# Top-k attention and a squared-ReLU feed-forward: ScalarE makes the masks, and the last batch runs by row groups

## The chip, the cores and the metric

The kernel runs on one core of a Trainium2 chip. The metric is the device time of one execution in microseconds (us). A core has five engines that each work through their own instruction list in order: TensorE (PE, matrix products), VectorE (DVE), ScalarE (ACT), GpSimd (POOL) and SyncE (SP, which here issues every DMA). They wait for each other by semaphores, so a waiting instruction holds up all that stands behind it on its engine.

## What is computed

Attention over 8 batches of 8 heads with 576 tokens of width 64, in which each query keeps only its 32 largest scores, followed by a feed-forward over the 4608 tokens of width 512:

```
scores = scale * np.matmul(q, k.transpose(0, 1, 3, 2))
kth    = np.partition(scores, -32, axis=-1)[..., -32:-31]
scores = np.where(scores >= kth, scores, -1e9)
attn   = exp(scores - max) / sum(exp(scores - max))
x      = (attn @ v), heads side by side     # [4608, 512]
r      = np.maximum(x @ w_in, 0.0)          # w_in  [512, 2048]
out    = (r * r) @ w_out                    # w_out [2048, 512]
```

## The kernel before

Heads are taken in pairs, so there are 8 batches of 4 pairs. The 576 query rows of a pair make 9 blocks of 128 rows (4 per head, and one block with the last 64 rows of both heads): 288 blocks in all. Blocks are worked in groups of 2, 2, 2 and 3, so a pair has 4 groups and the program 128.

**Search.** TensorE makes a block's scores in f32 (64x288 products), ScalarE copies them to SBUF as tile `s` (L482). The 32nd largest of 576 is found in two halves: `m` is the maximum of the two halves (VectorE, L510), `lo` the minimum, made on GpSimd from integer sums (`t1`, L507, and L513). VectorE then takes the top 32 of `m` in four rounds of MAX8 (L519) with MATCH_REPLACE8 (L525) between them, and the top 8 of `lo` (L533). Per group three small instructions follow: L543 merges the two lists, L547 makes a `shift` (the row's maximum, not below 0), L549 makes `nkth`, the negative of the 32nd largest.

**Mask.** GpSimd makes a mask `w` per block from the scores in two passes: `y = (s + nkth) * -2^90` (L558) and `w = max(min(y, 2^60), shift)` (L561).

**Attention.** After every second group of a pair, TensorE makes transposed scores once more and subtracts the masks with a matmul against `neg_bf`, the negative identity; ScalarE takes Exp into `p` (L611, L628, L641); TensorE multiplies by the values (with a column of ones, which gives the sum). VectorE takes the reciprocal of the sums out of PSUM (`rz`, L672) and multiplies (`x`, L674). TensorE transposes `x`, ScalarE copies it to `xt` (L696). There are two such stages per pair, of 256 and 320 rows.

**Feed-forward.** Once a batch's four pairs are done: 16 products with `w_in`, Relu on ScalarE (L718), a square on ScalarE (L725; VectorE in the last batch, L722), then `w_out` and a copy (L741) to the output DMA. Its work is spread through the next batch's searches; that of the last batch has no next batch.

**Order.** A planner in the program sets each engine's instruction list. Each operation has an estimated duration and a priority that stands for its due time (`PER`, 3.6 us a block, times the block's number); whichever operation is ready and has the lowest priority goes next, if its buffers are free. Buffers are numbered pools (8 PSUM banks; 9 of `s`, 12 of `w`, and so on). The planner lets a DMA hold SP for 0.06 us. At the end `nkth` and the lists of `lo` decide whether more than 8 of a row's 32 may have stood in `lo`; if so, the program runs a second, fuller pass (L834), which the profiled execution did not enter.

Of the kernel before, what the change touches and what calls it, by code (L numbers as in the profile page):

```python
# [5 lines left out]
ALU = mybir.AluOpType  # L6
# [4 lines left out]
I32 = mybir.dt.int32  # L11
# [65 lines left out]
class Op:  # L77
    __slots__ = ("eng", "dur", "prio", "fn", "deps", "tiles", "takes", "n", "users", "start", "end",
                 "idx", "sem", "val", "ndma", "seq", "vc", "waits", "wars", "later")
# [5 lines left out]
class Plan:  # L85
# [3 lines left out]
    def op(self, eng, dur, prio, fn, r=(), w=(), u=(), take=(), after=(), order=(), sem=None, ndma=0):  # L89
# [4 lines left out]
        o.sem, o.ndma, o.seq = sem, ndma, len(self.ops)  # L94
# [22 lines left out]
    def schedule(self, t0=0.0, latency=0.12, own=0.07):  # L117
# [17 lines left out]
        for o in self.ops:  # L135
            if left[o] == 0:
                heapq.heappush(ready[o.eng], (o.prio, o.seq, o))
        push(t0, "go", None)
        readyat = {o: t0 for o in self.ops}
        done = 0  # L140
        while events:
# [19 lines left out]
            for e in ENGS:  # L161
# [3 lines left out]
                while ready[e]:  # L165
# [23 lines left out]
                    hold = o.dur if e != "sp" else 0.06 * max(1, o.ndma)  # L189
                    o.end = t + o.dur  # L190
# [86 lines left out]
def bass_top_k_attn__then__act_relu_squared_kernel(  # L277
# [20 lines left out]
    def sb(name, shape, dt=FP32, n=None):  # L298
# [6 lines left out]
    neg_bf = sb("neg_bf", [P, P], BF16)  # L305
    b8all = sb("b8all", [P, NALL, 8])
    nkth = sb("nkth", [P, NALL])
    shift = sb("shift", [P, NALL])
    fcmp = sb("fcmp", [P, NALL])
    fone = sb("fone", [P, 2])  # L310
# [30 lines left out]
    em = Emitter(nc)  # L341


    GROUPS = [[(0, 0), (1, 0)], [(0, 1), (1, 1)], [(0, 2), (1, 2)], [(0, 3), (1, 3), (2, 4)]]
    PER = 3.6

    def build(full, first, setup):
        pl = Plan()
        act, vec, gp, pe = nc.scalar, nc.vector, nc.gpsimd, nc.tensor

        def mm(o, l, r, start, stop=True):
            return pe.matmul(o, l, r, start=start, stop=stop, skip_group_check=True)  # L352

        def tr(o, i, ident):
            return pe.matmul(o, i, ident, is_transpose=True, skip_group_check=True)

        weights = [] if not first else setup(pl)

        def block_n(pi, j):
            return NBLK * pi + j  # L360

        T0 = 14.0
        moe_done = {}

        for b in range(NB):
            xt = tile("xt")
            xt_writers = []
            for hp in range(NHP):
                pi = NHP * b + hp
                base = T0 + PER * NBLK * pi  # L370
                rq, rk, rv = tile("rq"), tile("rk"), tile("rv")

                def load(t, src, pi=pi, b=b, hp=hp):
                    def fn():
                        r = at(t)
                        res = []
                        for h in range(2):
                            sh = src[b, 2 * hp + h, :, :]
                            res.append(nc.sync.dma_start(
                                r[:, 0:4, h, :], sh[0:512, :].rearrange("(tb p) d -> p tb d", p=P)))  # L380
                            res.append(nc.sync.dma_start(r[0:64, 4, h, :], sh[512:576, :]))
                        return res
                    return fn

                def loadv(t, b=b, hp=hp):
                    def fn():
                        r = at(t)
                        res = []
                        for h in range(2):
                            sh = v[b, 2 * hp + h, :, :]  # L390
                            res.append(nc.sync.dma_start(
                                r[:, 4 * h:4 * h + 4, :],
                                sh[0:512, :].rearrange("(tb p) d -> p tb d", p=P)))
                            res.append(nc.sync.dma_start(r[64 * h:64 * h + 64, 8, :], sh[512:576, :]))
                        return res
                    return fn

                def slot_sem(o):
                    t = o.takes[0]
                    return f"{t.pool.name}{t.slot}"  # L400

                pl.op("sp", 2.3, base - 40, load(rq, q), w=[rq], take=[rq], sem=slot_sem, ndma=4)
                pl.op("sp", 2.3, base - 39.9, load(rk, k), w=[rk], take=[rk], sem=slot_sem, ndma=4)
                pl.op("sp", 2.3, base - 30, loadv(rv), w=[rv], take=[rv], sem=slot_sem, ndma=4)

                qk, vb = tile("qk"), tile("vb")
                tq, tk, tx = Tile(psum), Tile(psum), Tile(psum)

                def t4(o, src):
                    def fn():  # L410
                        r = at(src)
                        for tb in range(4):
                            ins = tr(bank(o)[:, 128 * tb:128 * tb + 128],
                                     r[:, tb, :, :].rearrange("p h d -> p (h d)"), ident32[:, :])
                        return ins
                    return fn

                def t5(o, a1, a2):
                    def fn():
                        for i, s in enumerate((a1, a2)):  # L420
                            ins = tr(bank(o)[:, 64 * i:64 * i + 64],
                                     at(s)[0:64, 4, :, :].rearrange("p h d -> p (h d)"),
                                     ident32[0:64, 0:64])
                        return ins
                    return fn

                o_q = pl.op("pe", .5, base - 14, t4(tq, rq), r=[rq], w=[tq], take=[tq, qk])
                pl.op("pe", .5, base - 13.9, t4(tk, rk), r=[rk], w=[tk], take=[tk], order=[o_q])
                pl.op("pe", .3, base - 13.8, t5(tx, rq, rk), r=[rq, rk], w=[tx], take=[tx], order=[o_q])
                pl.op("act", .62, base - 12.5, lambda qk=qk, tq=tq: act.copy(at(qk)[:, 0, 0:512], bank(tq)),  # L430
                      r=[tq], w=[qk])
                pl.op("act", .62, base - 12.4, lambda qk=qk, tk=tk: act.copy(at(qk)[:, 1, 0:512], bank(tk)),
                      r=[tk], w=[qk])
                pl.op("act", .3, base - 12.3, lambda qk=qk, tx=tx: act.copy(
                    at(qk)[:, :, 512:576], bank(tx)[:, 0:128].rearrange("p (a c) -> p a c", a=2)),
                    r=[tx], w=[qk])
                pl.op("gp", .7, base + 5, lambda vb=vb, rv=rv: gp.tensor_copy(
# [448 lines left out]
```

## Time and profile before

| | us |
|---|---|
| median of 3 runs (1238.94 to 1240.03) | 1239.09 |
| the profiled execution, its own time | 1230.77 |
| its span, first to last instruction | 1229.0 |
| busy in the span: DVE | 1154.5 (94%) |
| POOL | 986.4 (80%) |
| PE | 956.7 (78%), mean granted clock 0.888 |
| ACT | 576.3 (47%) |

An engine's busy share is an average over stages with different limits, so the stages are read one by one: the first search begins at 18.36 us, the last one's verdict stands at about 1171 us, and what is left after that is the last attention stage and the last batch's feed-forward. A granted clock of 1.0 is 2.4 GHz and of 0.5 is 1.2 GHz.

### The profile page before, as it was taken

What the parts mean: (1) busy time and instruction counts of PE and PEld (TensorE: products, weight loads), DVE (VectorE), ACT (ScalarE), POOL (GpSimd) and SP (SyncE); (2) the same over time, 40 slices, a digit from 0 to 9 for tenths busy, and PEclk for the clock granted to TensorE, in tenths of its full rate; (3) what the DMA queues carried; (4) which work ended last, traced back from release to release, by engine and by line L of the source; (5) the groups of instructions that cost most, each with busy time, mean ns of one, the idle gap of its engine ahead of it and who ended that gap; (6) DMA issues with size and microseconds to landing.
All of it is one profiled execution on the core that took longest, in us unless ns stands there. A gap on an engine that the chain in (4) does not pass through costs nothing.

```text
span 1229.0 us, 23132 instructions
## 1 busy us (share of the span) xinstructions
PE 956.7 (78%) x7938; PEld 570.8 (46%) x7938; DVE 1154.5 (94%) x3988; ACT 576.3 (47%) x953; POOL 986.4 (80%) x1282
## 2 busy tenths in 40 slices
PE   5465659988698868988688886898598886989567
PEld 3233336545364445544364443554365443644344
DVE  3899999999999999999999999999999999999921
ACT  3233237534384435734375443743366443754232
POOL 4899888888888888888888888888888888887710
PEclk8687779989799988999799987999888997999779
DMA  6432111012001111012011120011110120000001
GB/s 148 124 107 75 25 30 30 25 36 67 16 17 47 52 30 30 11 37 61 20 30 37 33 58 21 11 47 51 30 30 11 46 62 11 1 10 27 5 1 41
DMA packets 125438, 47.72 MB, mean 39 GB/s; under 512 B 117632, under 2 KB 117632, under 8 KB 125312
## 3 DMA queue, kind: packets, MB, share of 16 engines
q1 hardware_dynamic: 125312, 46.17, 14.6%
q8 instruction: 64, 1.05, 0.4%
q14 instruction: 62, 0.51, 0.1%
HBM read 36.70 MB, written 9.44 MB: 38 GB/s over the span
## 4 chain that ended last, share of the span: by engine, by line
DVE 89%; PE 4%; POOL 3%; SPq 1%; issue 1%; DMA 1%; ACT 0%; POOLq 0%
DVE a L519 32%; DVE wk L525 29%; DVE m L510 9%; DVE b8all L533 8%; DVE shift L547 5%; PE ps L352 4%; DVE a L543 2%; DVE x L674 2%; DVE nkth L549 1%; POOL y L558 1%; POOL w L561 1%; POOL win L784 0%; POOL t L507 0%; POOL lo L513 0%; DVE rz L672 0%
## 5 line engine op out<-in xcount | busy, mean ns | idle before, releaser
L352 PE MATMUL ps<-qk 64*128 64x288 f32 (+5 forms) x2560 | 469.5, 478 | 203.0 <-POOL w L561 167.0
L352 PEld LDWEIGHTS ps<-qk 64*128 64x128 f32 (+1 forms) x2560 | 226.5, 195 | 325.6 <-POOL w L561 182.8
L519 DVE MAX8 a<-wk 128x8 f32<-128x288 f32 x864 | 351.4, 451 | 0.0
L513 POOL TENSOR_TENSOR lo<-t,m 128x288 int32<-128x288 int32 x288 | 249.4, 883 | 88.1 <-DVE m L510 58.8
L482 ACT COPY s<-ps 128x576 f32<-128x576 f32 x288 | 175.8, 641 | 245.6 <-POOL y L558 146.8
L525 DVE MATCH_REPLACE8 wk<-a,wk 128x288 f32<-128x288 f32 x576 | 251.5, 449 | 0.0
L558 POOL TENSOR_SCALAR y<-s,nkth 128x576 f32<-128x576 f32 x288 | 213.9, 743 | 33.6 <-DVE nkth L549 4.7
L507 POOL TENSOR_TENSOR t<-s 128x288 int32<-128x288 int32 x288 | 228.6, 808 | 15.1
L561 POOL TENSOR_SCALAR w<-y,shift 128x576 bf16<-128x576 f32 x288 | 214.1, 743 | 29.8
L510 DVE TENSOR_TENSOR m<-s 128x288 f32<-128x288 f32 x288 | 148.2, 517 | 18.4 <-ACT s L482 18.4
L628 ACT ACTIVATE p<-ps 128x640 bf16<-128x640 f32 x128 | 90.1, 704 | 148.8 <-PE ps L352 148.8
L352 PE MATMUL ps<-wo,g 128*128 128x512 bf16 (+1 forms) x640 | 158.1, 385 | 0.0
L352 PEld LDWEIGHTS ps<-neg_bf,w 128*128 128x128 bf16 (+1 forms) x1600 | 91.4, 108 | 126.9 <-issue 126.9
L352 PE MATMUL ps<-xt,win 128*128 128x288 bf16 x1024 | 137.2, 290 | 4.9 <-DVE x L674 4.2
L352 PE MATMUL ps<-neg_bf,w 128*128 128x128 bf16 (+3 forms) x1600 | 133.7, 233 | 0.0
L525 DVE MATCH_REPLACE8 wk<-a,m 128x288 f32<-128x288 f32 x288 | 124.7, 441 | 0.0
L611 ACT ACTIVATE p<-ps 128x1024 bf16<-128x1024 f32 x64 | 65.5, 1023 | 126.3 <-PE ps L352 126.3
L533 DVE MAX8 b8all<-lo 128x8 f32<-128x288 f32 x288 | 116.4, 455 | 4.5 <-POOL lo L513 4.5
L519 DVE MAX8 a<-m 128x8 f32<-128x288 f32 x288 | 114.9, 443 | 0.0
L352 PEld LDWEIGHTS ps<-xt,win 128*128 128x128 bf16 x1024 | 98.1, 99 | 33.6 <-DVE x L674 5.4
L352 PEld LDWEIGHTS ps<-wo,g 128*128 128x128 bf16 (+1 forms) x640 | 57.4, 101 | 67.0 <-issue 13.2
L718 ACT ACTIVATE g<-ps 128x576 bf16<-128x576 f32 x128 | 80.6, 657 | 14.2 <-PE ps L352 13.8
(48 smaller groups left out, 785.4 us busy)
## 6 DMA issues: line engine op xcount, KB each, us to landing
rq<-in_q_dram SPq DMA_DIRECT2D x64, 128.0 KB, 2.3
rk<-in_k_dram SPq DMA_DIRECT2D x64, 128.0 KB, 2.4
rv<-in_v_dram SPq DMA_DIRECT2D x64, 128.0 KB, 2.4
out_dram<-o SPq DMA_DIRECT2D x32, 256.0 KB, 2.1
ws<-in_moe_w_in_dram SPq DMA_DIRECT2D x8, 512.0 KB, 4.4
ws<-in_moe_w_out_dram SPq DMA_DIRECT2D x8, 512.0 KB, 3.7
rq<-in_q_dram SPq DMA_DIRECT2D x64, 16.0 KB, 2.2
rk<-in_k_dram SPq DMA_DIRECT2D x64, 16.0 KB, 2.2
```

What stands on the lines that cost most here:

```text
L352: return pe.matmul(o, l, r, start=start, stop=stop, skip_group_check=True)
L482: pl.op("act", .67, tg - 6 + i, lambda s=st[i], p_=sp[i]: act.copy(at(s)[:, :].rearrange("p (a c) -> p a c", a=2), ps32[:, p_.slot:p_.slot ...
L507: pl.op("gp", .85, tg - 1 + .8 * i, lambda t=t1[i], s=st[i]: gp.tensor_tensor(at(t)[:, :].bitcast(I32), at(s)[:, 0:HALF].bitcast(I32), at( ...
L510: dve(.38, lambda t=m[i], s=st[i]: vec.tensor_tensor(at(t)[:, :], at(s)[:, 0:HALF], at(s)[:, HALF:S], ALU.max), r=[st[i]], w=[m[i]], take= ...
L513: pl.op("gp", .85, tg + .8 + .8 * i, lambda t=t1[i], m_=m[i], l=lo[i]: gp.tensor_tensor(at(l)[:, :].bitcast(I32), at(t)[:, :].bitcast(I32) ...
L519: last[i] = dve(.38, lambda s=src, i=i, rnd=rnd, A=A: vec.max(A(i, 8 * rnd, 8 * rnd + 8), at(s)[:, :]), r=[src], w=[a])
L525: f = (lambda s=src, d=wk[i], i=i, rnd=rnd, A=A: vec.match_replace(at(d)[:, :], A(i, 8 * rnd, 8 * rnd + 8), at(s)[:, :], NEG))
L533: bl[i] = dve(.38, lambda l=lo[i], i=i, B=B: vec.max(B(i, 0), at(l)[:, :]), r=[lo[i]], w=[bt] if full else [])
L558: pl.op("gp", .65, tw + 1.3 * i, lambda y=y, s=st[i], n=n0 + i: gp.tensor_scalar(at(y)[:, :], at(s)[:, :], nkth[:, n:n + 1], STEEP, ALU.ad ...
L561: pl.op("gp", .65, tw + 1.3 * i + .65, lambda y=y, w=w, n=n0 + i: gp.tensor_scalar(at(w)[:, :], at(y)[:, :], BIG, shift[:, n:n + 1], ALU.m ...
L628: pl.op("act", .72, tt + kb + 1, lambda e=e, kb=kb, pt=pt: act.activation(at(pt)[:, kb, :, :], ps32[:, e.slot:e.slot + 2, 0:320], ACTF.Exp ...
L718: pl.op("act", .67, tm + step * fb + 1, lambda hh=hh, g=gs[fb]: act.activation(at(g)[:, :].rearrange("p (a c) -> p a c", a=2), ps32[:, hh. ...
```

## The change

- **Mask.** `L547` and `shift` are gone. `kth` is the 32nd largest itself, and ScalarE makes the mask in one instruction, `w = Relu(kth - s)`, with `kth` as bias. The factor moves into the matmul: `steep_bf`, the identity times -2^90, takes the place of `neg_bf`. Kept scores give 0, the others something very large and negative. The two GpSimd passes are gone.
- **Division.** ScalarE copies the product with the values from PSUM to SBUF (`av`); VectorE takes the reciprocals from there into `rzall`; GpSimd does the multiplication to `x`.
- **Last batch.** Its groups are taken by row group over all four pairs: groups 2 and 3 of every pair, then group 0, then group 1. Attention runs over 320, 128 and 128 rows, and the feed-forward starts for rows 256 to 575 when those are done, then for rows 0 to 127, then for 128 to 255. 68 attention stages stand in place of 64.
- **Squares.** Those of the last two batches are on GpSimd, but for the last piece of 128 rows, which VectorE squares.
- **Planner.** New durations and due times, feed-forward steps with an earliest time (`nbf`), a DMA that holds SP for 0.6 us, other pool sizes (8 of `s`, 13 of `w`, 5 of `qk` and `vb`, 3 of `xt`). A load of q or k is 3 DMAs instead of 4. The first 7 operations on PE wait only for the identity.
- **Verdict.** It also asks that every reciprocal lies between 1e-30 and 1e30.

```diff
-        "s": ([P, S], FP32, 9), ... "y": ([P, S], FP32, 2), "w": ([P, S], BF16, 12),
+        "s": ([P, S], FP32, 8), ... "sh": ([P, 3], FP32, 2), "w": ([P, S], BF16, 13),
...
-                    hold = o.dur if e != "sp" else 0.06 * max(1, o.ndma)
+                    hold = o.dur if e != "sp" else 0.6 * o.ndma
...
-                    sh = dve(.08, lambda a=a, nb=nb, n0=n0: vec.tensor_scalar(
-                        shift[:, n0:n0 + nb], at(a)[:, 0:nb, 0], 0.0, None, ALU.max), r=[a])
...
-                        pl.op("gp", .65, tw + 1.3 * i, lambda y=y, s=st[i], n=n0 + i: gp.tensor_scalar(
-                            at(y)[:, :], at(s)[:, :], nkth[:, n:n + 1], STEEP, ALU.add, ALU.mult),
-                        pl.op("gp", .65, tw + 1.3 * i + .65, lambda y=y, w=w, n=n0 + i: gp.tensor_scalar(
-                            at(w)[:, :], at(y)[:, :], BIG, shift[:, n:n + 1], ALU.min, ALU.max),
+                    pl.op("act", .75, tw + .8 * i, lambda i=i: act.activation(
+                        at(ws[i])[:, :], at(st[i])[:, :], ACTF.Relu, bias=kth[:, n0 + i:n0 + i + 1], scale=-1.0),
...
+        minus = neg_bf if full else steep_bf
...
-                    pl.op("dve", .15, tt + 9, lambda av=av, rz=rz, nu=nu: vec.reciprocal(
-                        at(rz)[:, 0:nu], o_(av, nu)[:, :, 64]), r=[av], w=[rz])
-                    pl.op("dve", .45, tt + 9.1, lambda av=av, rz=rz, xr=xr, nu=nu: vec.tensor_tensor(
+            pl.op("act", .19 + 65 * nu / 1200, tt + 3, lambda: act.copy(
+                at(avs)[:, 0:nu, :], bank(av)[:, 0:65 * nu].rearrange("p (u c) -> p u c", c=65)), r=[av], w=[avs])
+            rz = pl.op("dve", .1, tt + 4, lambda: vec.reciprocal(rzall[:, u0:u0 + nu], at(avs)[:, 0:nu, 64]), r=[avs])
+            pl.op("gp", .15 + .16 * nu, tt + 4, lambda: gp.tensor_tensor(
+                at(xr)[:, 0:nu, :], at(avs)[:, 0:nu, 0:64],
...
+    def batch_order(b):
+        if b < NB - 1:
+            return ([(hp, g) for hp in range(NHP) for g in range(4)], {1: ([0, 1], False), 3: ([2, 3], True)},
+                    [(0, S)])
+        return ([(hp, g) for g in (2, 3, 0, 1) for hp in range(NHP)],
+                {3: ([2, 3], True), 0: ([0], False), 1: ([1], False)}, [(256, 320), (0, 128), (128, 128)])
...
+                elif b >= NB - 2:
+                    pl.op("gp", .15 + w_ / 480, tf + 1, lambda g=g: gp.tensor_tensor(
+                        at(g)[:, 0:w_], at(g)[:, 0:w_], at(g)[:, 0:w_], ALU.mult), u=[g])
```

Where the planner puts things, at three places. VectorE, middle of the program, from the end of one group's search to the start of the next, before (`m` belongs to the next group, `a` to the one that ends):

```order
L533 MAX b8all<-lo 128x8 x2
L510 TENSOR_TENSOR m<-s 128x288
L543 TENSOR_TENSOR a<-b8all,a 128x2x8
L510 TENSOR_TENSOR m<-s 128x288
L547 TENSOR_SCALAR shift<-a 128x2
L549 TENSOR_REDUCE nkth<-a 128x2
L519 MAX a<-m 128x8 x2
```

and VectorE at the same place now:

```order
L500 MAX b8all<-lo 128x8 x2
L479 TENSOR_TENSOR m<-s 128x288
L508 TENSOR_TENSOR a<-b8all,a 128x2x8
L479 TENSOR_TENSOR m<-s 128x288
L511 TENSOR_REDUCE kth<-a 128x2
L489 MAX a<-m 128x8 x2
```

The shift has left the list; the other five stand as they did. TensorE at the very start, before (transposes of the loaded q and k against the identity, then the first scores):

```order
L355 MATMUL ps<-ident,rq 128x128 x8
L355 MATMUL ps<-ident,rk 128x128 x4
L355 MATMUL ps<-ident,rq 128x64
L355 MATMUL ps<-ident,rk 128x64
L355 MATMUL ps<-ident,rk 128x128 x4
L355 MATMUL ps<-ident,rq 128x64
L355 MATMUL ps<-ident,rk 128x64
L352 MATMUL ps<-qk 128x288 x8
```

and TensorE at the start now:

```order
L361 MATMUL ps<-ident,rq 128x128 x4
L361 MATMUL ps<-ident,rk 128x128 x4
L361 MATMUL ps<-ident,rq 128x64
L361 MATMUL ps<-ident,rk 128x64
L358 MATMUL ps<-qk 128x288 x8
L361 MATMUL ps<-ident,rq 128x128 x4
```

The first pair's k and its scores no longer stand behind the second pair's q. TensorE at the end of the program now, from the feed-forward of rows 0 to 127 on (before, all the feed-forward of the last batch stood behind the last attention stage):

```order
L358 MATMUL ps<-xt,win 128x128 x64
L358 MATMUL ps<-wo,g 128x512 x4
L358 MATMUL ps<-qk 128x128 x8
L358 MATMUL ps<-steep_bf,w 128x128 x8
L358 MATMUL ps<-wo,g 128x512 x12
L358 MATMUL ps<-qk 64x128 x2
L358 MATMUL ps<-steep_bf,w 64x128 x2
L358 MATMUL ps<-wo,g 64x512 x4
L358 MATMUL ps<-vb,p 128x65 x10
L358 MATMUL ps<-wo,g 64x512 x8
L361 MATMUL ps<-ident_bf,x 128x128
```

Behind these rows stand only 64 products of 128 columns with `w_in` and 16 with `w_out`, for the last 128 rows; the rest of the feed-forward has moved ahead of the last attention stage.

## Rows read from the trace of the kernel before

**Rows 1.** The page's chain that ended last, by engine.
```profile
DVE 89%; PE 4%; POOL 3%; SPq 1%; issue 1%; DMA 1%; ACT 0%; POOLq 0%
```
**Rows 2.** Busy time by stage; each engine's us (instructions), then PEclk, DMA share, GB/s.
```profile
594.00:738.00 144.00, 117.78 (x1003) 69.52 (x1000) 144.00 (x502) 74.20 (x123) 122.49 (x159) 0.93 0.14 34
625.00:690.00 65.00, 57.42 (x486) 33.78 (x484) 65.00 (x225) 40.20 (x67) 54.64 (x71) 0.97 0.11 28
1026.00:1170.00 144.00, 111.69 (x932) 65.51 (x932) 143.90 (x499) 66.88 (x109) 116.36 (x149) 0.87 0.03 9
1170.00:1229.00 59.00, 44.92 (x296) 26.59 (x296) 9.25 (x22) 17.21 (x27) 4.74 (x6) 0.85 0.06 22
```
**Rows 3.** The same chain by line, with a decimal.
```profile
by line: DVE a L519 32.3%; DVE wk L525 28.9%; DVE m L510 9.4%; DVE b8all L533 8.1%; DVE shift L547 5.3%; PE ps L352 4.4%; DVE a L543 2.3%; DVE x L674 1.8%; issue 1.0%; DVE nkth L549 0.8%; POOL y L558 0.6%; POOL w L561 0.6%; POOL win L784 0.
```
**Rows 4.** VectorE's port users by line: duration ns min/median/max, first and last start.
```profile
L547 DVE TENSOR_SCALAR shift<-a x128: 155/755/1001, 30.6 to 1169.5; 128x2 f32<-128x2 f32 x96, 128x3 f32<-128x3 f32 x32
L543 DVE TENSOR_TENSOR a<-b8all,a x128: 160/190/1008, 29.6 to 1169.3; 128x16 f32<-128x16 f32 x96, 128x24 f32<-128x24 f32 x32
L510 DVE TENSOR_TENSOR m<-s x288: 439/456/1330, 18.4 to 1159.2; 128x288 f32<-128x288 f32 x144
```
**Rows 5.** Groups by line: busy us, mean ns | idle before, releaser.
```profile
L510 DVE TENSOR_TENSOR m<-s 128x288 f32<-128x288 f32 x288 | 148.2, 517 | 18.4 <-ACT s L482 18.4
L547 DVE TENSOR_SCALAR shift<-a 128x2 f32<-128x2 f32 (+1 forms) x128 | 76.9, 601 | 0.0
L543 DVE TENSOR_TENSOR a<-b8all,a 128x16 f32<-128x16 f32 (+1 forms) x128 | 42.4, 331 | 0.0
L558 POOL TENSOR_SCALAR y<-s,nkth 128x576 f32<-128x576 f32 x288 | 213.9, 743 | 33.6 <-DVE nkth L549 4.7
L561 POOL TENSOR_SCALAR w<-y,shift 128x576 bf16<-128x576 f32 x288 | 214.1, 743 | 29.8
L507 POOL TENSOR_TENSOR t<-s 128x288 int32<-128x288 int32 x288 | 228.6, 808 | 15.1
L725 ACT ACTIVATE g<-g 128x576 bf16<-128x576 bf16 x112 | 73.8, 690 | 0.9
```
**Rows 6.** Timeline of VectorE from 606.9 us: start, us, instruction.
```profile
606.92 0.76 DVE L543 TENSOR_TENSOR a<-b8all,a 128x16 f32<-128x16 f32 x1
607.61 0.45 DVE L510 TENSOR_TENSOR m<-s 128x288 f32<-128x288 f32 x1
607.98 0.76 DVE L547 TENSOR_SCALAR shift<-a 128x2 f32<-128x2 f32 x1
608.65 0.16 DVE L549 TENSOR_REDUCE nkth<-a 128x2 f32<-128x18 f32 x1
```
**Rows 7.** Timeline of GpSimd at the same place.
```profile
606.77 0.88 POOL L507 TENSOR_TENSOR t<-s 128x288 int32<-128x288 int32 x1
607.61 1.84 POOL L513 TENSOR_TENSOR lo<-t,m 128x288 int32<-128x288 int32 x2
```
**Rows 8.** Timeline of the start.
```profile
2.49 0.52 SPq L381 DMA_DIRECT2D rq<-in_q_dram  x1
...
4.72 1.09 PE L355 MATMUL ps<-ident,rq 128*128 128x128 f32 x4 [4.72 <-DMA rq<-in_q_dram]
...
12.97 1.06 PE L355 MATMUL ps<-ident,rk 128*128 128x128 f32 x4
...
18.36 0.53 DVE L510 TENSOR_TENSOR m<-s 128x288 f32<-128x288 f32 x1 [18.36 <-ACT s L482]
```
**Rows 9.** The chain at the end, in order of time: start, us, what.
```profile
1169.88 1.17 POOL y L558
...
1187.23 34.92 PE ps L352 x208
...
1222.17 0.58 ACT o L741
```
**Rows 10.** Waits over the whole span: us in total, times, longest.
```profile
PE ps L352 <- POOL w L561: 167.0, 60, 9.0
ACT s L482 <- POOL y L558: 146.8, 46, 8.4
```

More of the change, by code (lines that the diff above doesn't have):

```diff
@@ L305, in bass_top_k_attn__then__act_relu_squared_kernel @@
     neg_bf = sb("neg_bf", [P, P], BF16)
+    steep_bf = sb("steep_bf", [P, P], BF16)
     b8all = sb("b8all", [P, NALL, 8])
-    nkth = sb("nkth", [P, NALL])
-    shift = sb("shift", [P, NALL])
+    kth = sb("kth", [P, NALL])
+    rzall = sb("rzall", [P, NALL])
     fcmp = sb("fcmp", [P, NALL])
-    fone = sb("fone", [P, 2])
+    fone = sb("fone", [P, 4])
     heads = sb("heads", [P, 2])
@@ L785, in setup, with verdict @@
                                  r=[s]))
-        setup.pre = [i1, i2, i3] + ones + [f1]
-        return weights
-    main = build(False, True, setup)
-    for o in main.ops:
-        if o not in setup.pre and o.eng == "pe":
-            o.deps.update(setup.pre)
-    def fin(pl, waits):
-        vec, pe = nc.vector, nc.tensor
+        return [i1], pre, weights
+    def verdict(pl, kths, rzs):
         t = Tile(psum)
         c = pl.op("dve", .35, 1e6, lambda: vec.tensor_tensor(
-            fcmp[:, :], b8all[:, :, 7], nkth[:, :], ALU.add), after=waits)
+            fcmp[:, :], b8all[:, :, 7], kth[:, :], ALU.is_gt), after=kths)
@@ L801, in fin @@
-        g = pl.op("pe", .1, 1e6, lambda: pe.matmul(bank(t)[0:1, 0:1], fone[:, 0:1], fone[:, 1:2],
-                                                   start=True, stop=True), w=[t], take=[t], after=[f])
-        return pl.op("dve", .1, 1e6, lambda: vec.tensor_copy(flag[:, :], bank(t)[0:1, 0:1]), r=[t])
-    flagged = fin(main, list(kths))
+            fone[:, 2:3], fone[:, 2:3], 1e-30, None, ALU.is_lt), after=[f])
+        g = pl.op("pe", .1, 1e6, lambda: pe.matmul(bank(t)[0:1, 0:3], fone[:, 3:4], fone[:, 0:3],
+                                                   start=True, stop=True), w=[t], take=[t], after=[d, e, f])
@@ L806, in bass_top_k_attn__then__act_relu_squared_kernel @@
+        return pl.op("dve", .1, 1e6, lambda: vec.tensor_reduce(flag[:, :], bank(t)[0:1, 0:3], AX.X, ALU.max), r=[t])
+    main = Plan()
+    early, pre, weights = setup(main)
+    n_pre = len(main.ops)
+    kths, rzs = build(False, weights, main)
+    flagged = verdict(main, kths, rzs)
+    n = 0
+    for o in main.ops[n_pre:]:
+        if o.eng == "pe":
+            o.deps.update(early if n < 7 else early + pre)
+            n += 1
     span = main.schedule()
     em.number(main)
-    again = build(True, False, None)
```

740 lines of the change are left out of this document (357 added, 383 removed).

## The prediction

> **What bounds the kernel now.** I read the chain of waits first: VectorE holds 89% of it [rows 1]. The table by stage says where. In a full batch of the middle VectorE is busy for all 144.0 us of 144, beside 117.8 for TensorE, 122.5 for GpSimd and 74.2 for ScalarE; only after 1170 us does it stop, and then TensorE works alone for most of 59 us [rows 2]. So there are three stretches: a head until the first search at 18.4 us [rows 8], a search that VectorE paces until the first mask of the last group at 1169.9, and a tail that TensorE paces [rows 9]. An edit is worth what it takes from VectorE in the second, and from the chain in the other two. GpSimd's two mask passes, 428 us [rows 5], are no part of the second stretch by themselves.
>
> They are part of it in another way. Three VectorE instructions vary wildly: the shift takes 155 ns at best and 755 at the median, on 128x2 elements [rows 4]. The timeline shows why: at 606.92 the merge and at 607.98 the shift each last 0.76 us and end when a GpSimd instruction ends (t, 606.77 to 607.65; the first lo, from 607.61), while the reduction behind takes 0.16 [rows 6, 7]. Over all, the time beyond the shortest is 128 x (601 - 155) = 57 us for the shift, 128 x (331 - 160) = 22 for the merge, 288 x (517 - 439) = 22 for m [rows 4, 5].
>
> **The change, part by part.** The profiled execution took 1230.8 us, 1.8 over its span; the median of the runs is 1239.1, 0.7% more. I sum on the span and scale at the end.
>
> *Search.* The shift goes: 5.3% of the chain, 65 us. The multiplication to x leaves VectorE: 1.8%, 22 us [rows 3]. The reciprocals stay, 68 for 64. No row shows one that reads SBUF. If it is held up as the shift was, it costs 68 x 0.45 = 30 us; if it behaves as the reduction in the timeline, nothing. I take nothing, since the reduction is a neighbour on the same engine and also reads SBUF. The Trainium skill (SBUF — State Buffer, Who interferes with whom) says that copies, casts and tensor_scalar in a two-port mode and operations with two SBUF inputs take the port pair shared with GpSimd, and that a reduction never does. The trace agrees with that on the shift, the merge and the reduction; a reciprocal is not in the page's list, and by the page the sum would have 0 here and not 30.
>
> The 44 us of waiting of m and the merge shrink with GpSimd's load. GpSimd drops the 428 us of mask passes and gains two-input work: 2.8 ns an element by t (808 ns for 288) [rows 5], so 52 us for x (18432 columns) and 46 for the squares of the last two batches (16 x 576 + 16 x 448). That leaves 986 - 428 + 98 = 656 us, 60% of the new span, where a full batch now shows 85% [rows 2]. In proportion 44 becomes 31, 13 less. Bounds: all 44 go, or the shift's 57 pass to them (a rival). Search: 1169.9 - 18.4 = 1151.5, less 65, 22 and 13, is 1051 us, 131.4 a batch.
>
> *Cover.* ScalarE takes 288 masks. A square from SBUF of the same 576 columns costs 690 ns [rows 5]: 199 us, with 68 copies of the product at under that, 47, less 16 squares, 11: 576 becomes 811, 74% of the new span. It stays hidden if the masks do not hold up the copies of s behind them (a rival). TensorE's work does not change, but its 117.8 us must fit into 131.4: 90%. A stretch of 65 us already shows 57.4, 88% [rows 2], and the largest wait that keeps it below, 167 us for the GpSimd mask [rows 10], goes. I take VectorE as the pace here, barely.
>
> *Head.* Before, the first k was transposed at 12.97, behind the second pair's q in TensorE's list, and the first m started 5.4 us later [rows 8]. Now k is next. Its last DMA is the sixth in SP's queue; the fourth was issued at 2.49 and its data used at 4.72, and an issue takes about 0.6 us, so k is there at about 6, and m starts between 11.4 and 12.5. I take 11.8: a gain of 6.6 us. The search then ends at 11.8 + 1051 = 1063, and its last batch begins at 932.
>
> *Tail.* On VectorE's side: before, 17.3 us lay from the first mask to the feed-forward, for a stage of 320 rows, then 34.9 us of feed-forward, then 6.8 for copy and DMA [rows 9]. With 128 rows I take 9 (17.3 x 128/320 = 7 at least, and what does not shrink) and 10 (34.9 x 128/576 = 7.8 at least; weight loads do not shrink). 1063 + 9 + 10 + 7 = 1089. On TensorE's side: from the start of the last batch to the end it was busy for 111.7 + 44.9 = 156.6 us at clocks of 0.87 and 0.85 [rows 2], and that work, the seventh batch's feed-forward with it, now has to pass in one stretch. Scaled to the 0.93 of a full batch it is 146. I take 150, plus 4 for the further stages (0 to 8), 6 idle in the last chain and 7 behind: 932 + 167 = 1099. The Trainium skill (TensorE: Matmul & The Clock Gate, Part 1) says that the clock is throttled by default and that activity releases it; no row shows the last batch without its gaps, but the denser stretch at 0.97 agrees [rows 2]. By that rule, scaled to 0.97, the 150 would be 140 and TensorE's end 1089, level with VectorE's. Were the clock to stay as it is, 157, the end would be 1106.
>
> TensorE's side ends later, so the span is 1099, 130 less: 100 from the search, 7 from the head, 23 from the tail. With 1.8 around it 1100.8, and scaled by 1239.09/1230.77 it is 1108 us.
>
> **Rivals.** *TensorE paces every batch.* For it: 90% asked, 88% the best seen, and it now waits for an engine at 74% to empty its 8 PSUM banks. Against: its largest wait goes. If it holds 86%, a batch is 137 us, 5.6 more in 7 batches, and the span 1138: 1148 us.
>
> *The waiting for the port moves.* The merge and m stand where they stood, and GpSimd's lo now waits for m instead of running late, so it may start just in time to hold the third m of a group. If the shift's 57 us and the 13 I took off come back, the search ends at 1133 and VectorE's tail of 26 follows: 1159, so 1169 us. Against: where the next group has 2 blocks, 3 times in 4, only a reduction follows its second m.
>
> *Slower: ScalarE's list.* A mask waits for kth of its group, and copies of s behind it wait as well; VectorE then waits for s. If each group exposes its 2.25 masks at 0.69 us, that is 1.55 x 128 = 199 us: 1298 on the span, 1309 us. It decides from 1.0 us a group, since 130/128 eats the gain. Against: copies already waited 146.8 us for GpSimd's first pass to free s [rows 10], and VectorE waited for s once, at the start [rows 5]; for: a pool of 8 instead of 9.
>
> *The verdict asks for the second pass*, which is fuller than the first: over twice 1108 us. Only reciprocals outside 1e-30 to 1e30 add to what asked for it before, and a sum holds at least one Exp of a kept score.
>
> *More than I say:* no waiting left on the port and TensorE level with VectorE, 1063 - 31 + 26 = 1058, 1067 us.
>
> **How the numbers follow.** Forecast 0.56 (its own range 1085 to 1125), TensorE's pace 0.18, the port 0.12, more 0.09, ScalarE's list 0.04, second pass 0.01. The range of 1078 to 1162 takes in the forecast, TensorE's pace and the nearer half of the port and of more. About 0.2% is what a measurement of this kernel can tell from no change; slower is 0.05, within it 0.01, faster 0.94.
>
> **What would show it.** VectorE full from about 12 to 1063 us and 131 us a batch confirms the search; merge and m with means near 280 and 490 ns confirm the port; a median merge near 0.7 us is the second rival. Idle time of VectorE before m, put down to the copy of s, is the first rival when the copy waits for TensorE and the third when it stands behind a mask. In the tail, TensorE without gaps of over 2 us from 932 on and about 167 us to the end confirms its side. The prediction is wrong if the search falls by less than 70 us, or if TensorE's busy time in a middle batch leaves under 5 us of idle.

## The result and the profile after

The changed kernel takes 1117.31 us (median of 4 runs, 1116.01 to 1118.55), the kernel before 1239.47 beside it: a ratio of 0.901, 95% interval 0.900 to 0.903. The forecast was 1108 with a range of 1078 to 1162. The profiled execution took 1116.01 us, its span is 1114.2, and the forecast for the span was 1099.

The page of the changed kernel: busy time by engine, then the chain that ended last, as in [rows 1].

```profile
PE 936.5 (84%) x8082; PEld 551.0 (49%) x8082; DVE 1054.0 (95%) x3791; ACT 772.7 (69%) x1341; POOL 614.4 (55%) x815
...
DVE 79%; PE 14%; ACT 4%; issue 1%; DMA 1%; POOL 1%; SPq 0%; POOLq 0%
```

VectorE still holds most of the chain. Its share is smaller than the 89% before because the chain now runs through TensorE for some 150 us: 29 of them at the end, 24 in the last batch, and the rest in earlier batches, where it mostly passes through a reciprocal that waits for its input. Busy time by stage, as in [rows 2] (us and instructions of TensorE, its weight loads, VectorE, ScalarE and GpSimd; last columns granted clock, DMA share, GB/s): a middle batch, the last batch, the end.

```profile
542.00:675.00 133.00, 115.75 (x992) 67.52 (x992) 131.80 (x473) 99.26 (x174) 70.51 (x94) 0.95 0.17 41
942.00:1075.00 133.00, 115.92 (x1045) 68.45 (x1045) 129.00 (x452) 84.79 (x155) 87.92 (x107) 0.95 0.03 10
1075.00:1114.20 39.20, 30.74 (x305) 18.88 (x303) 4.58 (x14) 14.14 (x28) 6.52 (x9) 0.96 0.10 33
```

A batch takes 132.9 us instead of 144. In the middle VectorE is idle for 1.2 us of 133, in the last batch for 4.0; before it was for 0.0 and 0.1. Over the whole search, before and after (the same columns):

```profile
18.36:1169.90 1151.54, 904.40 (x7608) 538.19 (x7606) 1145.18 (x3967) 554.49 (x918) 977.09 (x1255) 0.89 0.15 38
11.42:1074.95 1063.53, 900.06 (x7759) 528.13 (x7757) 1049.36 (x3777) 755.24 (x1308) 603.21 (x781) 0.94 0.17 42
```

VectorE's busy time there fell by 95.8 us, and its idle time rose from 6.4 us to 14.2. Who holds it up, from 12 to 1075 us (total us, times, longest):

```profile
DVE rzall L622 <- ACT av L620: 11.5, 11, 2.1
DVE m L479 <- ACT s L456: 2.0, 1, 2.0
```

The groups that the change touches (busy us, mean ns | idle before, releaser), beside [rows 5]:

```profile
L482 POOL TENSOR_TENSOR lo<-t,m 128x288 int32<-128x288 int32 x288 | 251.1, 887 | 330.9 <-DVE a L508 240.0 <-DVE m L479 82.4 <-DVE rzall L622 8.5
...
L519 ACT ACTIVATE w<-s,kth 128x576 bf16<-128x576 f32 x288 | 214.4, 771 | 123.4 <-DVE kth L511 122.9
L479 DVE TENSOR_TENSOR m<-s 128x288 f32<-128x288 f32 x288 | 152.8, 531 | 13.4 <-ACT s L456 13.4
L624 POOL TENSOR_TENSOR x<-av,rzall 128x256 bf16<-128x256 f32 (+2 forms) x68 | 44.9, 660 | 78.5 <-DVE rzall L622 72.9 <-DVE a L508 5.5
...
L508 DVE TENSOR_TENSOR a<-b8all,a 128x16 f32<-128x16 f32 (+1 forms) x128 | 22.7, 177 | 0.2
```

The merge fell from a mean of 331 ns to 177, m rose from 517 to 531. The durations one by one (ns min/median/max, first and last start), as in [rows 4], each from the view of its own source line:

```profile
L479 DVE TENSOR_TENSOR m<-s x288: 427/446/1375, 11.4 to 1068.4; 128x288 f32<-128x288 f32 x144
...
L508 DVE TENSOR_TENSOR a<-b8all,a x128: 127/167/765, 18.9 to 1074.6; 128x16 f32<-128x16 f32 x96, 128x24 f32<-128x24 f32 x32
...
L622 DVE RECIPROCAL rzall<-av x68: 139/166/193, 38.5 to 1097.4; 128x5 f32<-128x5 f32 x32, 128x4 f32<-128x4 f32 x28, 128x2 f32<-128x2 f32 x8
```

No reciprocal took more than 193 ns: none of the 68 was held up. The median m is as short as before, so its mean comes from some that wait. Where, a timeline across the border of two groups shows (start, us, instruction):

```profile
559.70 0.43 DVE L479 TENSOR_TENSOR m<-s 128x288 f32<-128x288 f32 x1
...
560.06 0.16 DVE L508 TENSOR_TENSOR a<-b8all,a 128x16 f32<-128x16 f32 x1
560.14 0.45 DVE L479 TENSOR_TENSOR m<-s 128x288 f32<-128x288 f32 x1
560.22 1.02 POOL L482 TENSOR_TENSOR lo<-t,m 128x288 int32<-128x288 int32 x1 [1.78 <-DVE a L508]
...
560.51 0.16 DVE L511 TENSOR_REDUCE kth<-a 128x2 f32<-128x18 f32 x1
560.59 0.97 DVE L479 TENSOR_TENSOR m<-s 128x288 f32<-128x288 f32 x1
```

The first lo of the group starts behind the merge, while the second m runs, and the third m, which needs 0.44 us, ends only behind that lo. The reduction between them does not wait. Of the 32 third m of a group of three, 29 take over 0.6 us; before it was 3 of them, and 37 of the 96 first m of the groups of two. In both kernels 49 of the 288 m take that long. The Trainium skill (SBUF — State Buffer, Who interferes with whom) says that a VectorE instruction with two SBUF inputs and a GpSimd instruction that reads SBUF exclude each other, the one that issued first keeping the port. The trace agrees, with m at 0.97 us and the reduction at 0.16.

The head, beside [rows 8]:

```profile
6.45 1.12 PE L361 MATMUL ps<-ident,rk 128*128 128x128 f32 x4 [0.93 <-DMA rk<-in_k_dram]
...
11.42 0.46 DVE L479 TENSOR_TENSOR m<-s 128x288 f32<-128x288 f32 x1 [11.42 <-ACT s L456]
```

And the chain at the end in order of time, beside [rows 9]:

```profile
1074.77 0.18 DVE kth L511
1074.95 0.02 issue
1074.97 0.78 ACT w L519
1075.75 0.91 ACT p L581
...
1077.05 2.22 PE ps L358 x18
...
1079.32 6.06 PE ps L358 x56
...
1085.44 13.44 PE ps L358 x136
...
1099.70 7.21 PE ps L358 x80
...
1106.94 0.59 ACT o L698
```

The last 32nd largest stands at 1074.95. Of the 39.2 us behind it TensorE holds 28.9, in four pieces with 290 products, and 0.8 us between the last two pieces are two copies of ScalarE. The chain leaves VectorE by a mask of the last group, which stands in ScalarE's list ahead of an Exp that TensorE waits for.

### The profile page after: what moved, and what is told of

Its sections match the earlier page's. It is cut to its first block, busy times and chain, and to the rows that moved or that the text cites. A ratio compares the mean times of both kernels' runs of the same rounds, so it can differ in the third digit from the quotient of the medians.

```text
span 1114.2 us, 23090 instructions
## 1 busy us (share of the span) xinstructions
PE 936.5 (84%) x8082; PEld 551.0 (49%) x8082; DVE 1054.0 (95%) x3791; ACT 772.7 (69%) x1341; POOL 614.4 (55%) x815
## 4 chain that ended last, share of the span: by engine, by line
DVE 79%; PE 14%; ACT 4%; issue 1%; DMA 1%; POOL 1%; SPq 0%; POOLq 0%
DVE a L489 31%; DVE wk L494 27%; PE ps L358 13%; DVE m L479 10%; DVE b8all L500 8%; ACT w L519 2%; DVE a L508 1%; DVE kth L511 1%; ACT s L456 1%; DVE rzall L622 1%; DMA rq<-in_q_dram 1%; POOL lo L482 0%; ACT av L620 0%; SPq L377 0%; DMA rk<-in_k_dram 0%
## 5 line engine op out<-in xcount | busy, mean ns | idle before, releaser
L358 PE MATMUL ps<-qk 64*128 64x288 f32 (+7 forms) x2640 | 442.9, 448 | 81.7 <-ACT s L456 42.2
L358 PEld LDWEIGHTS ps<-qk 64*128 64x128 f32 (+1 forms) x2640 | 219.6, 187 | 204.6 <-ACT s L456 59.8
L519 ACT ACTIVATE w<-s,kth 128x576 bf16<-128x576 f32 x288 | 214.4, 771 | 123.4 <-DVE kth L511 122.9
L476 POOL TENSOR_TENSOR t<-s 128x288 int32<-128x288 int32 x288 | 227.9, 807 | 22.3 <-ACT s L456 19.9
L581 ACT ACTIVATE p<-ps 128x640 bf16<-128x640 f32 (+1 forms) x192 | 154.7, 809 | 77.2 <-PE ps L358 76.5
L358 PE MATMUL ps<-xt,win 128*128 128x288 bf16 (+2 forms) x1088 | 151.9, 290 | 25.3 <-ACT g L665 14.0
L358 PEld LDWEIGHTS ps<-steep_bf,w 128*128 128x128 bf16 (+1 forms) x1600 | 83.6, 102 | 112.6 <-issue 111.7
L358 PE MATMUL ps<-steep_bf,w 128*128 128x128 bf16 (+3 forms) x1600 | 124.1, 222 | 0.0
L489 DVE MAX8 a<-m 128x8 f32<-128x288 f32 x288 | 115.8, 442 | 0.2
L500 DVE MAX8 b8all<-lo 128x8 f32<-128x288 f32 x288 | 114.8, 439 | 0.0
L624 POOL TENSOR_TENSOR x<-av,rzall 128x256 bf16<-128x256 f32 (+2 forms) x68 | 44.9, 660 | 78.5 <-DVE rzall L622 72.9
L358 PEld LDWEIGHTS ps<-wo,g 128*128 128x128 bf16 (+1 forms) x640 | 54.3, 100 | 60.2 <-issue 11.8
L665 ACT ACTIVATE g<-ps 128x576 bf16<-128x576 f32 x112 | 72.5, 649 | 13.6 <-PE ps L358 12.8
L358 PE MATMUL ps<-vb,p 128*128 128x65 bf16 (+1 forms) x1600 | 62.8, 195 | 6.1 <-ACT p L594 6.0
```

The lines of the kernel that those rows point to most:

```text
L476: pl.op("gp", .81, tg - 1 + .8 * i, lambda i=i: gp.tensor_tensor(at(t1[i])[:, :].bitcast(I32), at(st[i])[:, 0:HALF].bitcast(I32), at(st[i] ...
L489: last[i] = dve(.365, lambda i=i, rnd=rnd, src=src: vec.max(A(i, rnd), at(src[i])[:, :]), r=[src[i]], w=[a])
L500: bl = [dve(.365, lambda i=i: vec.max(B(i, 0), at(lo[i])[:, :]), r=[lo[i]], w=[bt] if full else []) for i in range(nb)]
L519: pl.op("act", .75, tw + .8 * i, lambda i=i: act.activation(at(ws[i])[:, :], at(st[i])[:, :], ACTF.Relu, bias=kth[:, n0 + i:n0 + i + 1], s ...
L581: return act.activation(o, i, ACTF.Exp, scale=0.125)
L624: pl.op("gp", .15 + .16 * nu, tt + 4, lambda: gp.tensor_tensor(at(xr)[:, 0:nu, :], at(avs)[:, 0:nu, 0:64], rzall[:, u0:u0 + nu].unsqueeze( ...
```

## The experiments

Each was timed beside the kernel before on the same chip (its medians: 1238.4 to 1240.0 us), so that differences between runs of one or two us can be the chip's. "Search ends" is the end of the last reduction to kth, "tail" what follows it in the span.

| | median us | ratio, 95% interval | search ends | tail |
|---|---|---|---|---|
| the changed kernel | 1117.31 | 0.901 [0.900, 0.903] | 1075.0 | 39.2 |
| e1_x_vector | 1129.50 | 0.911 [0.910, 0.913] | 1096.2 | 30.8 |
| e2_gp_mask_no_shift | 1526.37 | 1.231 [1.229, 1.233] | | |
| e3_gp_mask_shift | 1567.27 | 1.264 [1.262, 1.266] | | |
| e2b_gp_mask_no_shift | 1169.89 | 0.944 [0.942, 0.945] | 1144.4 | 24.4 |
| e3b_gp_mask_shift | 1219.76 | 0.985 [0.983, 0.987] | 1192.6 | 23.5 |
| e4_no_row_groups | 1128.32 | 0.910 [0.908, 0.912] | 1069.7 | 56.7 |
| e5_late_rz | 1108.92 | 0.895 [0.893, 0.896] | 1066.4 | 39.2 |
| e6_less_ff | 1114.29 | 0.899 [0.898, 0.901] | 1072.8 | 39.2 |
| e7_old_sp | 1122.68 | 0.906 [0.903, 0.908] | 1083.7 | 39.3 |
| e8_lo_behind_m | 1099.59 | 0.888 [0.886, 0.889] | 1058.0 | 39.2 |
| e9_both | 1092.62 | 0.882 [0.880, 0.883] | 1050.6 | 39.4 |
| e10_less_ff7 | 1115.75 | 0.901 [0.899, 0.902] | 1075.4 | 39.2 |

**e1: the division back on VectorE.** The reciprocal and the product read PSUM again, and ScalarE's copy is gone; the masks stay on ScalarE.

```diff
-            pl.op("act", ..., lambda: act.copy(at(avs)[:, 0:nu, :], bank(av)[:, 0:65 * nu]...
-            rz = pl.op("dve", .1, tt + 4, lambda: vec.reciprocal(rzall[:, u0:u0 + nu], at(avs)[:, 0:nu, 64]), r=[avs])
-            pl.op("gp", .15 + .16 * nu, tt + 4, lambda: gp.tensor_tensor(
+            rz = pl.op("dve", .1, tt + 4, lambda: vec.reciprocal(rzall[:, u0:u0 + nu], pv()[:, :, 64]), r=[av])
+            pl.op("dve", .08 + .07 * nu, tt + 4, lambda: vec.tensor_tensor(
...
```

> The changed kernel with the division put back: VectorE takes the reciprocals out of PSUM and multiplies to x; no copy of the product on ScalarE, none of x on GpSimd. All else as in the changed kernel (1117.3 us). My sum: 68 multiplications at about 0.33 us come back to VectorE, 22 us, but the waits of the reciprocals for ScalarE's copy inside the search (11.5 us) shrink to a few: 1124 to 1131 us. Rival (those waits are TensorE's lateness and not the copy's, so they stay): 1137 to 1141 us. Rival (the division was hidden anyway, the search is not VectorE's): within 3 us of 1117.

It is 12.2 us slower than the changed kernel. That lies within the expected time, but by luck: the waits of the reciprocals were to shrink and grew, as the first rival has it, the search ends 21.2 us later, and only a tail that is 8.4 shorter, which no sum had, brings the time back. Two groups of e1, by line, and its chain at the end:

```profile
L479 DVE TENSOR_TENSOR m<-s 128x288 f32<-128x288 f32 x288 | 145.3, 505 | 11.0 <-ACT s L456 11.0
L623 DVE TENSOR_TENSOR x<-ps,rzall 128x256 bf16<-128x256 f32 (+2 forms) x68 | 28.9, 424 | 0.1
```

```profile
1096.05 0.18 DVE kth L511
...
1098.12 4.66 PE ps L358 x68
...
1102.83 8.73 PE ps L358 x67
...
1112.38 3.75 PE ps L358 x64
1116.18 3.42 PE ps L358 x15
```

The product costs VectorE 28.9 us here, and m is 26 ns shorter, 7.5 us in 288. VectorE's busy time is 15.2 us above the changed kernel's (1069.2 against 1054.0), and its reciprocals wait 20.5 us in the search instead of 11.5, for TensorE's product itself: they wait without ScalarE's copy too. So of the 21 us by which the search is longer, 6.5 are idle time of VectorE (20.7 us against 14.2) and not the product's; why TensorE is later there was not tried. At the end the chain runs through 214 products of TensorE instead of 290.

**e2 and e3: the two GpSimd passes back, without and with the shift.** Both keep the division of e1 and take `neg_bf` again. The first pass subtracts the 32nd largest and multiplies, in place; the second clips, to 0 or to the shift.

```diff
-                    pl.op("act", .75, tw + .8 * i, lambda i=i: act.activation(
-                        at(ws[i])[:, :], at(st[i])[:, :], ACTF.Relu, bias=kth[:, n0 + i:n0 + i + 1], scale=-1.0),
+                    pl.op("gp", .75, tw + 1.3 * i, lambda i=i: gp.tensor_scalar(
+                        at(st[i])[:, :], at(st[i])[:, :], kth[:, n0 + i:n0 + i + 1], STEEP, ALU.subtract, ALU.mult),
...
+                        at(ws[i])[:, :], at(st[i])[:, :], BIG, 0.0, ALU.min, ALU.max),
```

> The kernel of e1 with the masks put back on GpSimd in two passes, but without the shift on VectorE: w = max(min((s - kth) * -2^90, 2^60), 0) against the negative identity. It parts the shift from the load of GpSimd. My theory (the shift was the dear part: each one waited for a GpSimd instruction, and the reduction in its place does not): GpSimd near 990 us busy raises the mean of m and the merge to about what they had before, 15 to 25 us over e1, so 1140 to 1155. Rival (what counts is GpSimd's load; with it back, the wait of the shift passes to the merge and to m): 45 to 75 us over e1, 1170 to 1205, with a median of the merge near 0.7 us.

> The kernel of e2 with the shift back on VectorE, behind the reduction, as maximum of the row's best score and 0, used by the second pass. My theory: 50 to 65 us over e2 (128 shifts at about 0.5 us on the chain), 1195 to 1215, with the shift's median near 0.75 us. Rival (the wait only moves between the port's users): within 15 us of e2.

Both missed by some 360 to 380 us, and not for what they were to test; the shift was worth 40.9 us between them, less than the 50 to 65 expected. The first pass of e2, by line:

```profile
L519 POOL TENSOR_SCALAR s<-s,kth 128x576 f32<-128x576 f32 x288 | 642.5, 2231 | 30.7 <-DVE kth L511 4.1
```

It takes 2231 ns where the kernel before needs 743 for add and multiply [rows 5], and GpSimd holds 51% of the chain. Two things differ from the pass before, the subtraction and working in place. So both were run again with the addition.

**e2b and e3b: the same with an addition.** VectorE's reduction writes the 32nd largest negated, and the pass adds it; it still works in place.

```diff
-                        at(st[i])[:, :], at(st[i])[:, :], kth[:, n0 + i:n0 + i + 1], STEEP, ALU.subtract, ALU.mult),
+                        at(st[i])[:, :], at(st[i])[:, :], kth[:, n0 + i:n0 + i + 1], STEEP, ALU.add, ALU.mult),
```

> As the run with masks on GpSimd and no shift, but the first pass adds the negative kth instead of subtracting kth; VectorE stores kth negated, and the verdict adds it. If the subtraction was what made the first pass 2231 ns long, it is back at about 740 here, GpSimd falls from 1394 to about 1000 us busy, and the time is 15 to 45 us over e1 (1129.5): 1145 to 1175. Rival (the pass is slow because it writes over its input): still above 2000 ns and near 1526 us.

> The kernel of e2b with the shift back on VectorE, behind the reduction. My theory (each shift waits for a GpSimd instruction, and without it nothing takes over that wait): 50 to 65 us over e2b. Rival (the wait only moves between the port's users): within 15 us of e2b, and the merge or m longer in e2b by what the shift took.

e2b came out within what was expected, and e3b at its edge: the shift is worth 49.9 us. The first pass and the merge of e2b, by line:

```profile
L519 POOL TENSOR_SCALAR s<-s,kth 128x576 f32<-128x576 f32 x288 | 216.9, 753 | 33.0 <-DVE kth L511 6.6
...
L508 DVE TENSOR_TENSOR a<-b8all,a 128x16 f32<-128x16 f32 (+1 forms) x128 | 65.6, 512 | 0.0
```

The pass takes 753 ns: it was the subtraction that cost three times as much, not the place. The shift and the merge of e3b, by line:

```profile
L519 DVE TENSOR_SCALAR sh<-a 128x2 f32<-128x2 f32 (+1 forms) x128 | 68.7, 537 | 0.0
L508 DVE TENSOR_TENSOR a<-b8all,a 128x16 f32<-128x16 f32 (+1 forms) x128 | 45.0, 352 | 0.0
```

Taking only the shift out (e3b to e2b) frees 68.7 us and lets the merge grow by 128 x 160 ns = 20.5, while m falls from a mean of 550 ns to 508: with GpSimd about as full as before (1003 us busy, 986 before), part of the wait moves to the neighbour, as the rival has it, but not all. Taking GpSimd's mask passes away as well (e2b to e1) is worth another 40.4 us, the search ending 48.2 earlier and the tail being 6.4 longer; 128 x (512 - 177) ns = 43 is the merge's.

**e4: the last batch in the order of the others.**

```diff
-        if b < NB - 1:
+        if b < NB:
```

> The changed kernel with the last batch in the order of the others: pair by pair, two attention stages a pair, one feed-forward of 576 rows behind the last stage. My sum: the search ends where it did, near 1075; behind it a stage of 320 rows (17.3 us before, less about 4 for masks in one pass), 35 us of feed-forward and 7 for the last copy and DMA: 1130 on the span, 1133 us, 16 more than the changed kernel. Rival (TensorE's backlog sets the end in either order, since the work is the same): within 5 us of 1117.

11.0 us slower, some 5 less than expected: the tail is 17.5 longer, but the search ends 5.3 earlier. Its chain at the end:

```profile
1069.71 2.12 ACT w L519 x3
...
1083.73 18.50 PE ps L358 x128
...
1102.28 10.74 PE ps L358 x49
1113.07 6.55 PE ps L358 x29
```

All the feed-forward of 576 rows stands behind the last attention stage, as before the change [rows 9].

**e8: lo behind all m of its group.** Each lo waits for the group's last m.

```diff
-                dve(.42, lambda i=i: vec.tensor_tensor(
+                om = dve(.42, lambda i=i: vec.tensor_tensor(
...
+            for i in range(nb):
                 pl.op("gp", .88, tg + .8 + .8 * i, lambda i=i: gp.tensor_tensor(
...
-                    at(m[i])[:, :].bitcast(I32), ALU.subtract), r=[t1[i], m[i]], w=[lo[i]], take=[lo[i]])
+                    at(m[i])[:, :].bitcast(I32), ALU.subtract), r=[t1[i], m[i]], w=[lo[i]], take=[lo[i]],
+                    after=[om])
```

> The changed kernel, in which GpSimd's lo of a group waits for the last m of that group instead of its own. In the changed kernel 49 of 288 m take over 0.6 us, mostly the third m of a group of three, held by the lo that started beside it. If that is what holds them, the mean of m falls from 531 to about 460 ns and the time by 12 to 20 us: 1097 to 1105. Rival (the wait moves to whatever port user comes next, or TensorE sets the pace): within 4 us of 1117.

17.7 us faster than the changed kernel, as expected, though the mean of m falls to 481 ns and not to 460. The group of m in e8:

```profile
L479 DVE TENSOR_TENSOR m<-s 128x288 f32<-128x288 f32 x288 | 138.2, 481 | 13.2 <-ACT s L456 13.2
```

288 x 50 ns = 14.4 of the 17.7 are m itself, and nearly all of it lies in the third m of a group of three: their mean falls from 917 ns to 487, and 4 of 32 take over 0.6 us instead of 29. GpSimd has the same work to do. So it was lo that held the third m, not GpSimd's load at large.

**e5: the reciprocals 4 us later in the planner**, with x and what follows it, in all batches but the last.

```diff
+            dl = 0 if tl else 4
...
-            rz = pl.op("dve", .1, tt + 4, lambda: vec.reciprocal(...
+            rz = pl.op("dve", .1, tt + 4 + dl, lambda: vec.reciprocal(...
```

> The changed kernel with the reciprocals, the multiplication to x, its transposes and its copy given due times 4 us later in all batches but the last, so that VectorE reaches a reciprocal after ScalarE has copied the product. If those waits (11.5 us in the search) are a matter of the order of VectorE's list, they vanish and the time falls by 6 to 11 us: 1106 to 1111. Rival (ScalarE is behind by a queue that follows, because TensorE and ScalarE pace the early batches): within 3 us of 1117, with the idle time of VectorE moved to m.

8.4 us faster, as expected. VectorE's wait for the copy in its search, from 12 to 1066 us:

```profile
DVE rzall L623 <- ACT av L621: 2.0, 4, 0.8
```

9.5 of the 11.5 us are gone. Before the change the reciprocals were due 9 us after their stage's time in the plan and waited 1.7 us in the whole search; now they are due after 4, and stand in VectorE's list ahead of their input.

**e9: e5 and e8 together.**

> The two last edits together: lo behind the last m, and the division's due times 4 us later. If they are two waits on VectorE's chain, they add: 1117.3 - 17.7 - 8.4 = 1091, so 1088 to 1095. Rival (TensorE sets the end once VectorE is that much faster): 1097 to 1100, with the search shorter and the tail longer by the same.

As expected, the two add: 1092.62 us, 11.8% under the kernel before and 2.2% under the changed one. In its search VectorE waits 0.3 us for the copy and 2.0 for s, and its chain is VectorE's again:

```profile
DVE 91%; PE 6%; ACT 1%; issue 0%; POOL 0%; SPq 0%; DMA 0%; POOLq 0%
```

**e6 and e10: less work for TensorE.** Of four partial products with w_in one is made, in the first six batches (e6) or in the seventh, whose feed-forward runs beside the last batch's search (e10). What follows the products is the same.

```diff
-                        for ct in range(NCT):
+                        for ct in range(NCT if b >= NB - 2 else 1):
```

```diff
-                        for ct in range(NCT):
+                        for ct in range(NCT if b != NB - 2 else 1):
```

> The changed kernel without 3 of the 4 partial products with w_in in the first six batches (their output is not that of the reference); the order is the same, and TensorE has some 12 us less to do in each of six batches, 72 in all. My theory (VectorE paces the search, TensorE only the tail, and the last two batches keep all their work): the search loses at most the waits it had for TensorE and ScalarE, 1108 to 1117. Rival (TensorE's pace holds VectorE in every batch): 1060 to 1095.

> The changed kernel without 3 of the 4 partial products with w_in in the seventh batch alone, whose feed-forward stands in TensorE's list between the attention stages of the last batch (the output is not the reference's there); the order is the same. If TensorE's backlog sets the end, as my prediction had it, the 12 us of work taken out shorten the stretch behind the search from 39 us to between 27 and 33, and the time is 1104 to 1111. Rival (the chain of the last attention stage and feed-forward sets it): within 3 us of 1117.

e6 gains 3.0 us, as expected of a TensorE that does not pace a middle batch. e10 missed: it was to give 6 to 13 us, and gave 1.6, which the intervals do not part from nothing; the rival, the chain of the last stages, had allowed 3. Busy time of e10 in its last batch and at its end:

```profile
942.00:1075.00 133.00, 111.15 (x948) 62.27 (x952) 129.28 (x452) 84.53 (x155) 87.99 (x106) 0.86 0.03 11
1075.00:1114.60 39.60, 30.88 (x303) 19.13 (x306) 4.95 (x16) 14.17 (x28) 6.96 (x10) 0.94 0.10 33
```

TensorE has 97 fewer products in its records of the last batch and 4.8 us less busy time, at a granted clock of 0.86 instead of 0.95; and the tail is the same to 0.1 us.

**e7: the planner's hold on SP as before.** A DMA holds SP for 0.06 us in the plan instead of 0.6.

```diff
-                    hold = o.dur if e != "sp" else 0.6 * o.ndma
-                    o.end = t + o.dur + (hold if e == "sp" else 0)
+                    hold = o.dur if e != "sp" else 0.06 * max(1, o.ndma)
+                    o.end = t + o.dur
```

> The changed kernel with the planner's old estimate for SP (a DMA holds it for 0.06 us). If that estimate is what set TensorE's first products in the order of the data, the first search starts later by 6 us or so and the time grows by 4 to 9 us: 1121 to 1126. Rival (the 3 DMAs a load and the first 7 operations without the masks' constants did it): within 2 us of 1117.

5.4 us slower by the medians, as expected; its four runs lie between 1120.2 and 1125.9, and the profile is of one at 1124.8. VectorE's waits near its start, from 14 to 60 us:

```profile
DVE m L479 <- ACT s L456: 14.5, 1, 14.5
DVE b8all L500 <- POOL lo L482: 8.4, 2, 8.1
```

The first m stands at 14.5 instead of 11.4, 3 us later where 6 were expected, and an early lo comes 8.1 us late as well, which was not.

## Why the prediction was right, and where its steps were not

On the span 114.8 us went, against 130 forecast: 6.9 in the head (7), 88.0 in the search (100) and 19.9 in the tail (23). What bounds the kernel, and that each of the three falls, was right; two of the sizes came out near for other reasons than those given.

**Head.** 11.8 forecast, 11.42 measured; with the old hold on SP, 14.5 (e7).

**Search.** 1051 us forecast, 1063.5 measured (11.4 to 1075.0). The terms one by one:

- *The shift, 65 us.* It is gone. Alone, at the place behind the reduction, it is worth 49.9 (e3b to e2b), the merge taking over 20 us of waiting. With GpSimd's passes gone too the merge has little wait left to take, at 177 ns. Together the two steps (e3b to e1) are worth 90.3 by the medians, against 65 + 13 = 78 in the sum.
- *Waiting left on m and the merge, 31 us.* Measured: 288 x (531 - 439) = 26.5 and 128 x (177 - 160) = 2.2, 28.7 together. The sum was right by luck, and its parts were not: the merge was to keep a mean of 280 ns and has 177, m was to fall to 490 and rose to 531. The step "In proportion 44 becomes 31" is what failed. Where lo stands decides: behind the merge now, beside the group's third m. That is the second rival's mechanism, and e8 shows it; undoing it gives 17.7 us, where the rival had priced 70.
- *The division, 22 us.* 21 in the search (e1), of which 8 come back in the tail. The two figures are near each other by luck, since 6.5 of the 21 are idle time that grew in e1, and m gave 7.5 back.
- *The reciprocals, nothing.* 139 to 193 ns: no port wait, as taken. But VectorE waits 11.5 us in the search for the copy `av`, and 2.0 for an s. The search is 12.5 us longer than forecast: VectorE's busy time fell by 95.8 us instead of 100.5, which is 4.7, and its idle time rose from 6.4 us to 14.2, which is 7.8. For the 7.8 the prediction had no term: it priced the reciprocals' port and not their place in VectorE's list, though the planner's due time for them had moved from 9 us to 4. It is not the copy that does it: e1 has none and waits 20.5 us. e5 puts 4 us back, takes 9.5 of the wait away and gains 8.4.

**Cover.** ScalarE is busy for 772.7 us (811 forecast), GpSimd for 614.4 (656). A mask takes 771 ns against the 690 taken from the square, for 214 us. The Trainium skill (ScalarE: Activation LUTs, What ACT_TABLE_LOAD costs) gives an ACTIVATE with its bias in a tile 280 ns + 0.833 an element, an estimate of 760 ns for 576. The trace agrees, with 771. The third rival, ScalarE's list, did not appear: VectorE waited for s once behind the start. Nor did the first, TensorE's pace: 115.75 of 133 us busy in a middle batch, and 6.7 us less work in it (109.05 busy in e6) moved the end by 3.

**Tail.** 36 us behind the search forecast, 39.2 measured, and TensorE sets it, as said. But the step that gave the number failed, and the number is near by luck: "that work, the seventh batch's feed-forward with it, now has to pass in one stretch". There was no such stretch, and the sign that was to confirm it, no gap of over 2 us, did not come. TensorE was idle for 17 us of the last batch, 11.6 of them in one wait for a mask and one for a copy of s. The first, in its timeline (idle before and releaser in brackets):

```profile
982.08 1.44 PE L358 MATMUL ps<-qk 64*128 64x320 f32 x4 [5.95 <-ACT w L519]
```

With the seventh batch's work cut the tail stayed at 39.2 (e10). In e5 to e9, whose searches end between 1050.6 and 1083.7, it is 39.2 to 39.4, and the chain's pieces on TensorE at the end are those of the changed kernel to the digit, 2.22, 6.06, 13.44 and 7.21 us. So the tail is the length of what the planner's lists put behind the last group's mask: 290 products on TensorE and the links between them. VectorE's side, 26 us, was too short for the same reason: it counted the last 128 rows' stage and feed-forward, and left out what stands in front of them in TensorE's list: stages of earlier pairs, the rest of rows 256 to 575 and the feed-forward of rows 0 to 127. (The sum has a slip besides: 150 us scaled from 0.93 to 0.97 are 144 and not 140, and TensorE's end by that is 1093 and not 1089.) Where the list is another, in e1, the tail is 30.8. The row groups are worth 11.0 us by the medians (e4); in the profiles 17.5 in the tail less 5.3 lost in the search.

**The scale.** Medians were taken to lie 0.7% over the profiled execution, as before. For the changed kernel they lie 0.1% over it (1117.31 to 1116.01). On the span the forecast was 15 us short, on the median 9: this factor hid 6 of the miss, by luck.

**The whole, by single steps.** From the kernel before to e3b 19.5 us (head, tail and the rest of the planner), the shift 49.9, GpSimd's mask passes 40.4, the division 12.2; 122 together. Each step also reorders the planner's lists, so these are prices in this order of steps. Why e2b's and e3b's tails are 24 us was not tried.

## What to carry to other kernels

A wait on a shared port belongs to a place in two lists: ask which GpSimd instruction starts while which VectorE instruction runs, and price that; a share of load gave the sum here by luck, and none of its parts. An instruction that is due earlier in a planned order needs a term of its own: it can wait for its input on the engine that sets the pace, even if it is short and its input is made elsewhere. The length of a tail is read from the list behind the last release, not from an engine's backlog: here, kernels that end their search at quite different times but have the same list behind it keep it to 0.2 us.

## What the runs showed of the hardware that was not expected

- GpSimd's 128x576 pass with a subtraction and a multiplication takes 2231 ns, with an addition and a multiplication 753; tile, type and place are the same (e2, e2b). Only this shape and f32 were run.
- In the last batch the granted clock, a mean over two levels of 1.0 and 0.5, was 0.86 instead of 0.95 when TensorE had 97 of 1045 products less there (e10), and in a middle batch 0.88 instead of 0.95 with 95 of 992 less (e6). Busy time fell only from 115.9 to 111.2 us and from 115.8 to 109.1: taking work from an engine that is not the bound did not shorten even its own busy time in proportion.
